# A transformer block in one kernel: jobs ordered by a table of ranks, input weights laid out piece by piece, a constant added inside a reduction

## The chip, the cores and the metric

The kernel runs on one core of a Trainium2 chip. The metric is the device time of one execution in microseconds (us); the median of several executions counts. The core has a matrix engine (TensorE, PE in the profile, with its weight loads as PEld), a vector engine (VectorE, DVE), an activation engine (ScalarE, ACT), a general engine (GpSimd, POOL) and SyncE (SP), which here issues every DMA. Each engine works through its own list of instructions in the order in which the program was written; semaphores hold an instruction until what it needs is done.

## The reference

```
scores = q @ k.T / 8, causal mask, softmax; attn = softmax @ v      # 4 batches, 12 heads, 448 positions, 64 wide
x  = attn, heads side by side                                       # 4 x 448 x 768
u  = x + (relu(x.T @ w_tok1) @ w_tok2).T                            # token mixing, 448 -> 256 -> 448
x  = u + relu(u @ w_ch1) @ w_ch2                                    # channel mixing, 768 -> 1536 -> 768
h  = relu(x @ w_in); a, v = halves of h                             # 768 -> 2 x 512
v  = (v - mean) / sqrt(var + 1e-6), over the 512 columns
out = (a * (w_spatial @ v + b_spatial)) @ w_out                     # 512 -> 768
```

Inputs of `q`, `k`, `v` are fp32; the weights arrive in 8-byte numbers and are narrowed to fp32 on the chip.

## The kernel before

Most products are made of three matmuls on fp32r operands: each operand is split into a high part (a cast, mostly on ACT) and a low part (the difference, on DVE or POOL), and high x high, high x low and low x high are summed in PSUM. That is `mm3` (lines 336 to 338), a helper, so that most matmuls of the profile carry one of these three lines. The low parts are made by `lo_part` (line 327) and the low part of a hidden value, with its relu, by `relu_lo` (line 330).

The work goes through these stages, which overlap. **Attention**: 24 pairs of heads; for each pair `scores` (matmuls, line 497; mask, scale and row maximum on DVE, line 506; exponential on ACT, line 523; the sum of a row gets 1e-9 added on DVE, line 534, and is inverted, line 535; rows are normalised on POOL, line 544), `transposed` (line 581, transposes on PE, copied out of PSUM on ACT or DVE, lines 585 and 584) and `weighted` (lines 669, 683 and 688). The last seven pairs are turned by DVE and a trip through DRAM instead. **Token mixing** follows every third pair (`token_mix`, with transposes on PE in line 741). **Weights**: a piece of the channel weights is loaded into the tile `way` (line 381), narrowed by three DVE instructions (`narrow`, lines 351, 353 and 355), stored to a DRAM tile `plain` (line 395), and later loaded again for a batch into a tile `whl` (`load_unit`, line 818), cast on ACT (line 819) and split on POOL (line 327). The gated part's weights go the same way (`gw`, lines 1105 and 1107). **Channel mixing** of batches 0 and 1 (`ch1`, with its relu on ACT in line 843 and `relu_lo` on DVE; `ch2`, whose result DVE adds to `U` in line 859), then of batches 2 and 3 together with seven products in place of eight (`seven`, `gather`, lines 997 to 1003 and 1080), then the gated part the same way, with the spatial product in lines 1355 and 1356 and its DVE steps in lines 1362 and 1363.

The order of the work is not that of the source. Every piece of work is a `Job` with an engine, a price in microseconds, the keys it reads and writes, the buffers it touches and a priority. `Plan.order` plays the jobs through a model of the engines (`Plan.run`): at each step it takes, among jobs that could start first, the one of the best priority. Priorities of the first pass come from formulas beside each job; then `Plan.due` walks backward from the end and gives each job its latest start as its priority, and the play is repeated, six passes in all (`PASSES`); the pass with the earliest end is used. In this model a DMA takes its bytes at 340 GB/s and 2.3 us more (`LANDING`), and a result reaches another engine after 0.1 to 0.25 us and PE 0.3 or 0.8 us later still. The play also picks PSUM banks, and for some copies whether ACT or DVE does them. The instructions of all five engines are then written out in the order of the modelled starts. Nothing is reordered on the chip.

Of the kernel before, what the change touches and what calls it, by code (L numbers as in the profile page):

```python
# [2 lines left out]

# [59 lines left out]
PASSES = 6  # L63
DUE = "ACT", "DVE", "POOL", "SP", "PE"
# [4 lines left out]
LANDING = 2.3  # L69

TOK_PRIO = 1.0

BLOCKS = 17


class Buf:


    def __init__(self, make, tag, prev=None, banks=None):
        self.make, self.tag, self.prev, self.banks = make, tag, prev, banks  # L80
        self.jobs, self.tile, self.left = [], None, 0

# [7 lines left out]
class Job:  # L90
    def __init__(self, eng, us, emit, prio, at, size, index, port, other):
        self.eng, self.us, self.emit, self.prio, self.at, self.size, self.index = eng, us, emit, prio, at, size, index
        self.other = other
        self.port = port or eng == "POOL"
        self.before, self.after, self.bufs = set(), [], set()


class Plan:
# [11 lines left out]
    def job(self, eng, us, emit, r=(), w=(), touch=(), prio=0.0, at=0.0, size=0, port=False, other=None):  # L110


        j = Job(eng, us, emit, prio, at, size, len(self.jobs), port, other)
# [16 lines left out]
        j.bufs |= set(touch)  # L130
        self.jobs.append(j)
        return j

    def order(self):
# [10 lines left out]
        own = {j: (j.eng, j.us, j.emit, j.prio) for j in self.jobs}  # L145
        best = None
        for k in range(PASSES):
            for j in self.jobs:
                j.eng, j.us, j.emit, _ = own[j]
            if not self.run():  # L150
                break
            end = max(j.start + j.us for j in self.jobs)
            if best is None or end < best[0]:
                best = end, [(j.start, j.eng, j.us, j.emit) for j in self.jobs], {b: b.tag for j in self.jobs for b in j.bufs if b.banks}
            self.due(end, own, k)
        for j, x in zip(self.jobs, best[1]):
            j.start, j.eng, j.us, j.emit = x
        for b, tag in best[2].items():
            b.tag = tag
        return sorted(self.jobs, key=lambda j: (j.start, j.index))  # L160

    def due(self, end, own, k):

        jobs = sorted(self.jobs, key=lambda j: (j.start, j.index))
        owners = {}
        for j in jobs:
            for b in j.bufs:
                if b.banks and b not in owners.setdefault(b.tag, []):
                    owners[b.tag].append(b)
        later = {}  # L170
        for l in owners.values():
            for b, c in zip(l, l[1:]):
                later[b] = [j for j in c.jobs if not j.before.intersection(c.jobs)]
        late, pe = {}, end
        for j in reversed(jobs):
            t = pe if j.eng == "PE" else end
            for a in j.after:
                lat = 0.0
                if a.eng != j.eng or j.eng == "SP":
                    lat = 0.25 if j.eng == "PE" else 0.1  # L180
                    if a.eng == "PE":
                        lat += 0.3 if j.start < START else 0.8
                if j.eng == "SP":
                    lat += j.size / 340e3 + LANDING
                t = min(t, late.get(a, end) - lat)
            for b in j.bufs:
                if j in b.jobs:
                    for a in later.get(b, ()):
                        t = min(t, late.get(a, end) - 0.3)
            late[j] = t - j.us  # L190
            if j.eng == "PE":
                pe = late[j]
        for j in self.jobs:
            if own[j][0] in DUE and own[j][3] < 1e8:
                j.prio = late[j]

    def run(self):
# [9 lines left out]
        free = dict.fromkeys(engines, 0.0)  # L207
        bank_free = [0.0] * 8
        dma = port_free = 0.0
        avail = {e: [] for e in engines}  # L210
# [8 lines left out]
        def start(j, e):  # L219
            s = max(free[e], j.ready, port_free if j.port else 0.0)  # L220
            for b in j.bufs:
                if b.banks and b.tag is None:
                    s = max(s, min(bank_free[i] for i in b.banks))
            return s

        done = 0
        while done < len(self.jobs):
            best = None
            for e in engines:
                if not avail[e]:  # L230
                    continue
                starts = [(start(j, e), j) for j in avail[e]]
                first = min(s for s, _ in starts)
                if first == inf:
                    continue
                s, j = min(((s, j) for s, j in starts if s <= first + 0.03), key=lambda x: (x[1].prio, x[1].index))
                if best is None or (s, j.prio) < (best[0] - 0.1, best[1].prio) or s < best[0] + 0.1 and j.prio < best[1].prio:
                    best = (s, j, e)
            if best is None:
                return False  # L240
# [6 lines left out]
            for b in j.bufs:  # L247
                if b.banks and b.tag is None:
                    b.tag = min(b.banks, key=lambda i: (bank_free[i] > s, -bank_free[i] if bank_free[i] <= s else bank_free[i]))
                    bank_free[b.tag] = inf  # L250
            j.start = s
            free[j.eng] = s + j.us
            if j.port:
                port_free = s + j.us
            end = s + j.us
            if j.eng == "SP":
                dma = max(dma, end) + j.size / 340e3
                end = dma + LANDING
            done += 1
            for b in j.bufs:  # L260
                if j in b.jobs:
                    b.left -= 1
                    if b.left == 0 and b.banks:
                        bank_free[b.tag] = end + 0.3
            for a in j.after:
                lat = 0.0
                if a.eng != j.eng or j.eng == "SP":
                    lat = 0.25 if j.eng == "PE" else 0.1
                    if a.eng == "PE":
                        lat += 0.3 if s < START else 0.8  # L270
                a.ready = max(a.ready, end + lat)
# [3 lines left out]
        return True  # L275
# [3 lines left out]
def mixer_kernel(ctx: ExitStack, tc: tile.TileContext, qkv, wtok, wch, wgv, wsp, bsp, out):  # L279
# [36 lines left out]
    def dve(n, psum=True):  # L316
        return (n * 1.05 + 60) / 1e3 if psum else (n * 1.09 + 40) / 1e3

    def pool(n, two=True):
        return (n * 2.35 + 60) / 1e3 if two else (n * 0.83 + 230) / 1e3  # L320
# [19 lines left out]
    def narrow(d, dk, w, wk, n, prio, banks=(3,)):  # L340
# [16 lines left out]
        for k in range(3):  # L357
            job("DVE", (n * 1.03 + 165) / 1e3, lambda k=k: step(k), r=[dk, (ps, 0)] if k else [dk], w=[wk] if k == 2 else [(ps, 0)], touch=[wk[0]], prio=prio)
# [10 lines left out]
    stats = [fixed(f"s{i}", [3, 8], F32, f"stats{i}") for i in range(4)]  # L369
# [5 lines left out]
    def convert(i, src, parts, prio, banks, keep=None):  # L375
# [5 lines left out]
        job("SP", 0.4, lambda: nc.sync.dma_start(b.t[:, : 2 * n], src.bitcast(U32)), w=[dk], prio=prio, size=n * 1024)  # L381
# [12 lines left out]
        if keep is not None:  # L394
            job("SP", 0.4, lambda: nc.sync.dma_start(plain[keep], b.t[:, 4 * HALF : 6 * HALF].bitcast(F32)), r=[(b, "w", x) for x in (False, True)], w=[("plain", keep)], prio=prio, size=393216)
# [1112 lines left out]
```

## Time and profile before

| | us |
|---|---|
| median of 3 executions | 760.67 |
| the three executions | 760.67, 758.09, 761.02 |
| the profiled execution, first to last instruction | 760.7 |
| PE busy in it | 747.2 |
| DVE busy | 622.3 |
| ACT busy | 427.4 |
| POOL busy | 298.2 |

The profiled execution's own time is its span: it agrees with the median of the three to a rounding, so nothing lies around the span that the trace doesn't show. The end of a matmul is modelled in the profile, and a matmul's row is longer than the distance to the next one, so PE's busy share hides short gaps; the distance between the starts of neighbours shows them.

### The profile page before, as it was taken

Reading aid. Unit: us, or ns where it says so; the run is one execution under the profiler, and the core shown is the slowest. Engines: PE = TensorE matmul, PEld = TensorE weight load, DVE = VectorE, ACT = ScalarE, POOL = GpSimd, SP = SyncE. Lnnn points to the kernel's source line nnn. Section 1 sums busy time; section 2 is a strip of 40 time slices with the busy share of each in tenths; the row PEclk is TensorE's granted clock in tenths of the full one; section 3 lists DMA queues with packets and bytes.
Section 4 is the critical chain, followed back from the end, with each engine's and each line's share of the span. In section 5 each row is a group of like instructions: output and inputs, shape, how many; then the busy total and the mean of one; then the engine's idle time right before and its main releaser. Section 6 shows DMA issues by size and latency. Waiting matters only on the chain. (4 is left out here: it accounts for less than half of the span.)

```text
span 760.7 us, 12440 instructions
## 1 busy us (share of the span) xinstructions
PE 747.2 (98%) x4216; PEld 640.3 (84%) x4216; DVE 622.3 (82%) x1512; ACT 427.4 (56%) x1040; POOL 298.2 (39%) x354
## 2 busy tenths in 40 slices
PE   8999999999989999999999999999999999999998
PEld 4577778888887888888889989998988888888997
DVE  6999599999867878876469978999999897599482
ACT  6998776445347765552336666654573665545241
POOL 4788764265494766563310000000420151542210
PEclk9999999999999999999999999999999999999999
DMA  6687158999976898898823122520301100400213
GB/s 228 207 285 238 55 163 316 335 318 333 339 225 190 298 307 250 234 304 220 241 84 117 39 84 84 187 84 1 118 22 42 43 0 1 132 1 28 83 49 133
DMA packets 48608, 122.02 MB, mean 160 GB/s; under 512 B 4896, under 2 KB 20256, under 8 KB 48032
## 3 DMA queue, kind: packets, MB, share of 16 engines
q1 hardware_dynamic: 48544, 121.23, 48.7%
q8 instruction: 33, 0.54, 0.3%
q14 instruction: 31, 0.25, 0.1%
HBM read 91.46 MB, written 29.75 MB: 159 GB/s over the span
## 5 line engine op out<-in xcount | busy, mean ns | idle before, releaser
L336 PE MATMUL psf<-fb,fa 128*128 128x448 f32 x420 | 154.0, 367 | 1.2 <-DVE hs L1001 0.6
L337 PE MATMUL psf<-fb,fa 128*128 128x448 f32 x420 | 153.7, 366 | 0.0
L338 PE MATMUL psf<-fb,fa 128*128 128x448 f32 x420 | 153.6, 366 | 0.0
L327 POOL TENSOR_TENSOR whl<-whl 128x768 fp32r<-128x768 f32 x45 | 83.2, 1851 | 89.5 <-ACT whl L819 89.4
L523 ACT ACTIVATE P<-P,stats 128x448 f32<-128x448 f32 (+3 forms) x192 | 96.1, 505 | 31.1 <-DVE stats L506 30.8
L544 POOL TENSOR_SCALAR P<-P,stats 128x448 f32<-128x448 f32 (+3 forms) x192 | 88.3, 483 | 38.1 <-DVE stats L535 30.8
L336 PEld LDWEIGHTS psf<-fb,fa 128*128 128x128 f32 x420 | 78.9, 188 | 9.2 <-DVE hs L1001 1.0
L337 PEld LDWEIGHTS psf<-fb,fa 128*128 128x128 f32 x420 | 78.9, 188 | 6.8
L338 PEld LDWEIGHTS psf<-fb,fa 128*128 128x128 f32 x420 | 78.9, 188 | 6.7
L506 DVE CUSTOM_DVE_ANT_0 P<-pss,mask 128x448 f32<-128x448 f32 (+3 forms) x192 | 70.9, 415 | 16.4 <-PE pss L497 16.0
L938 ACT CAST fa<-raw 128x384 fp32r<-128x384 f32 (+1 forms) x112 | 56.4, 531 | 42.7 <-DVE raw L951 21.6
L327 POOL TENSOR_TENSOR wv<-wf,wv 128x512 fp32r<-128x512 f32 x6 | 9.2, 1546 | 153.2 <-ACT wv L1156 153.2
L327 DVE TENSOR_TENSOR fa<-raw,fa 128x384 fp32r<-128x384 f32 (+1 forms) x109 | 61.0, 585 | 7.1 <-ACT fa L938 7.1
L336 PE MATMUL ps<-hid,whl 128*128 128x448 f32 x144 | 55.2, 383 | 3.1 <-DVE hid L330 1.9
L819 ACT CAST whl<-whl 128x768 fp32r<-128x768 f32 x45 | 37.4, 833 | 34.6 <-DMA whl<-plain 33.5
L336 PE MATMUL ps<-uhl,whl 128*128 128x448 f32 x144 | 55.6, 386 | 0.2 <-DVE U L859 0.2
L338 PE MATMUL ps<-hid,whl 128*128 128x448 f32 x144 | 53.3, 370 | 0.0
L337 PE MATMUL ps<-hid,whl 128*128 128x448 f32 x144 | 53.3, 370 | 0.0
L338 PE MATMUL ps<-uhl,whl 128*128 128x448 f32 x144 | 52.7, 366 | 0.0
L337 PE MATMUL ps<-uhl,whl 128*128 128x448 f32 x144 | 52.7, 366 | 0.0
L859 DVE TENSOR_TENSOR U<-ps,U 128x448 f32<-128x448 f32 x48 | 29.5, 619 | 20.9 <-PE ps L338 20.8
L327 POOL TENSOR_TENSOR ql<-stage,qh 128x896 fp32r<-128x896 f32 x18 | 38.1, 2116 | 14.9 <-issue 11.7
(174 smaller groups left out, 1793.2 us busy)
## 6 DMA issues: line engine op xcount, KB each, us to landing
way<-in_wch SPq DMA_DIRECT2D x24, 768.0 KB, 5.7
whl<-plain SPq DMA_DIRECT2D x45, 384.0 KB, 5.0
stage<-in_qkv SPq DMA_DIRECT2D x23, 448.0 KB, 4.7
plain<-way SPq DMA_DIRECT2D x24, 384.0 KB, 6.7
raw<-plain SPq DMA_DIRECT2D x24, 384.0 KB, 3.9
round<-PB SPq DMA_DIRECT2D x7, 1024.0 KB, 6.2
PT<-round SPq DMA_DIRECT2D x28, 256.0 KB, 6.2
v<-in_qkv SPq DMA_DIRECT2D x24, 256.0 KB, 4.1
```

Of the source, the lines that this page charges most:

```text
L327: e.tensor_tensor(lo, x, hi.bitcast(F32), op=ALU.subtract)
L336: nc.tensor.matmul(ps, ah, bh, start=(first and i == 0), stop=False, **kw)
L337: nc.tensor.matmul(ps, ah, bl, start=False, stop=False, **kw)
L338: nc.tensor.matmul(ps, al, bh, start=False, stop=(last and i == n - 1), **kw)
L506: nc.vector.tensor_tensor_reduce(out=P(i)[:M, j, :], in0=ps(i, j), in1=mask[:M, S - 128 : S - 128 + W] if j == 0 and n < BLOCKS or M == 64 ...
L523: nc.scalar.activation(P(i)[:M, j, :], P(i)[:M, j, :], AF.Exp, bias=s.t[:M, 0, c : c + 1], scale=-1.0, accum_out=s.t[:M, 1, c : c + 1])
L544: nc.gpsimd.tensor_scalar(P(i)[:M, j, :], P(i)[:M, j, :], s.t[:M, 2, c : c + 1], 1.0, op0=ALU.mult, op1=ALU.mult)
L819: job("ACT", act(DM, False), lambda: nc.scalar.copy(w.t[:, 0, :], w.t[:, 1, :].bitcast(F32)), r=ks, w=ks, prio=p)
L859: job("DVE", dve(S), lambda d=d, ps=ps: nc.vector.tensor_tensor(u.t[:, d, :], ps.t[:, :S], u.t[:, d, :], op=ALU.add), r=[(ps, 0), *u_keys( ...
L938: job("ACT", act(n, False), lambda: nc.scalar.copy(part(o, 0), at(d)), r=[key(d)], w=[wk], prio=p + 0.1 * o)
```

## The change

Three things are changed. First, the order: the six passes and `due` are removed, and each job's priority is read from a table of ranks, one number for each job, written into the source as text (`RANKS`); one play of the model follows. The model itself gets other prices: how late a result reaches each engine from each other one (`LAG`), a DMA's bytes at 290 to 415 GB/s behind a fixed 1.35 or 2.2 us from its issue, and for PE a kind of matmul for each job (`mode`: fp32r products and transposes 0, scores 1, weighted sums 2), with 0.09 us for a change of kind, a `lead` for the first product after a change or a wait, and a preference of 1.0 (`STAY`) for a job of the kind at hand. Prices of single jobs are set anew. Which instructions there are stays as it was, but for the choices that the play makes (bank, ACT or DVE) and the third part below.

Second, the layout in DRAM of three inputs. `in_wch`, `in_wgv` and `in_wtok` were arrays of 128 rows, and a piece was a range of columns of each row (rows of `in_wch` lie 147,456 bytes apart, and a piece takes 6,144 bytes of each); now each piece lies in one block. Sizes of the loads stay.

Third, the 1e-9 of the softmax's sum. Before, a DVE `tensor_scalar_add` (line 534) added it. Now the exponential writes its row sums into every second column of a strip, whose other columns are set to 1e-9 once at the start (four more small POOL memsets), and a DVE `tensor_reduce` adds neighbours; the reciprocal follows as before.

```
+STAY, NEAR, SLACK = 1.0, 0.03, 0.2
+LAG = {
+    "DVE": {"DVE": 0.123, "ACT": 0.118, "POOL": 0.168, "PE": 0.138, "SP": 0.11},
+    "ACT": {"DVE": 0.133, "ACT": 0.0, "POOL": 0.18, "PE": 0.155, "SP": 0.126},
...
+RANKS = (
...
-        own = {j: (j.eng, j.us, j.emit, j.prio) for j in self.jobs}
-        best = None
-        for k in range(PASSES):
...
-            self.due(end, own, k)
...
+        ranks = array("H", b85decode("".join(RANKS)))
+        assert len(ranks) == len(self.jobs)
+        for j, r in zip(self.jobs, ranks):
+            j.prio = r / 40
+        self.run()
         return sorted(self.jobs, key=lambda j: (j.start, j.index))
...
+            return min(((s, j) for s, j in starts if s <= first + NEAR), key=lambda x: (x[1].prio + (e == "PE" and x[1].mode != mode) * STAY, x[1].index))
...
+            if e == "PE":
+                waited = s > free[e] + 0.03
+                if j.mode != mode and not waited:
+                    s += 0.09
+                if j.mode == 0 and (waited or mode):
+                    us += j.lead
+                mode = j.mode
...
-            if j.eng == "SP":
-                dma = max(dma, end) + j.size / 340e3
-                end = dma + LANDING
+            if e == "SP":
+                free[e] = s + 0.385
+                dma = end = max(dma, s + (1.35 if j.mode else 2.2)) + j.size / (j.lead * 1e6)
...
-    stats = [fixed(f"s{i}", [3, 8], F32, f"stats{i}") for i in range(4)]
+    stats = [fixed(f"s{i}", [4, 8], F32, f"stats{i}") for i in range(4)]
+
+    def sums(s):
+        return s.t[:, 2:4, :].rearrange("p x c -> p (x c)").rearrange("p (c x) -> p c x", x=2)
...
-                nc.vector.tensor_scalar_add(s.t[:, 2, cols], s.t[:, 1, cols], 1e-9)
-                nc.vector.reciprocal(s.t[:, 2, cols], s.t[:, 2, cols])
+                nc.vector.tensor_reduce(s.t[:, 1, cols], sums(s)[:, cols, :], axis=mybir.AxisListType.X, op=ALU.add)
+                nc.vector.reciprocal(s.t[:, 1, cols], s.t[:, 1, cols])
...
+    def piece(x, o, n):
+        return x[128 * o : 128 * (o + n)].rearrange("(p n) -> p n", n=n)
...
-        convert(i % 3 if i < 6 else 1 + i % 2, wch[:, i * DM : i * DM + DM], parts, LOW + i, (7,) if i < 8 else (3,), keep=i)
+        convert(i % 3 if i < 6 else 1 + i % 2, wch[i], parts, LOW + i, (7,) if i < 8 else (3,), keep=i)
...
     for s in stats:
         nc.gpsimd.memset(s.t, 0.0)
+        nc.gpsimd.memset(sums(s)[:, :, 1:2], 1e-9)
...
-    wch = np.concatenate([first[u[1]] if u[0] == 1 else second[u[1], u[2]] for u in UNITS], axis=1)
+    wch = np.stack([first[u[1]] if u[0] == 1 else second[u[1], u[2]] for u in UNITS])
...
+    wgv = in_pieces(wgv, [HALF] * 8 + [FF] * KM + [HALF] * 8)
+    wtok = in_pieces(wtok, (768, 704, 448))
```

## Rows read from the trace of the kernel before

**Rows 1.** The page: span, and busy time of the matrix engine

```profile
span 760.7 us, 12440 instructions
PE 747.2 (98%) x4216; PEld 640.3 (84%) x4216; DVE 622.3 (82%) x1512; ACT 427.4 (56%) x1040; POOL 298.2 (39%) x354
```

**Rows 2.** Stretches: length, busy PE, PEld, DVE, ACT, POOL; clock, DMA share, GB/s

```profile
20.00:50.00 30.00, 28.40 (x219) 18.70 (x216) 27.39 (x108) 30.00 (x96) 24.09 (x45) 1.00 0.76 251
...
100.00:215.00 115.00, 111.74 (x658) 94.56 (x658) 106.25 (x252) 60.19 (x145) 61.25 (x68) 0.99 0.89 308
500.00:600.00 100.00, 99.43 (x471) 88.02 (x471) 97.93 (x207) 53.24 (x120) 14.04 (x18) 1.00 0.16 50
```

**Rows 3.** Who PE waited for: idle us in total, times, longest

```profile
PE ps L336 <- DVE U L859: 1.2, 2, 1.1
PE psp L1355 <- DVE gate L1363: 0.9, 2, 0.7
...
PE psf L336 <- DVE hs L1001: 0.6, 1, 0.6
PE psf L336 <- DVE U L1080: 0.6, 1, 0.6
```

**Rows 4.** Timeline, all engines, about the longest wait: start, length, instruction, [idle before]

```profile
208.00 0.36 PE L338 MATMUL ps<-uhl,whl 128*128 128x448 f32 x1
...
209.82 0.37 PE L338 MATMUL ps<-hid,whl 128*128 128x448 f32 x1
210.02 0.83 ACT L819 CAST whl<-whl 128x768 fp32r<-128x768 f32 x1 [1.93 <-DMA whl<-plain]
210.76 0.54 ACT L843 ACTIVATE hid<-ps 128x448 fp32r<-128x448 f32 x1
...
211.45 0.62 DVE L330 SCALAR_TENSOR_TENSOR hid<-ps,hid 128x448 fp32r<-128x448 f32 x1
...
212.13 0.47 PE L336 MATMUL ps<-hid,whl 128*128 128x448 f32 x1 [1.94 <-DVE hid L330]
...
212.43 0.36 PE L337 MATMUL ps<-hid,whl 128*128 128x448 f32 x1
```

**Rows 5.** The stretch right behind that wait; columns as in the other stretches

```profile
213.10:216.50 3.40, 3.40 (x11) 3.05 (x10) 3.25 (x7) 2.59 (x4) 3.40 (x6) 0.50 0.58 201
```

**Rows 6.** Timeline of PE: first and last change of kind, and two changes

```profile
4.09 1.18 PE L497 MATMUL pss<-stage 64*64 64x64 f32 x8
...
184.73 0.37 PE L338 MATMUL ps<-hid,whl 128*128 128x448 f32 x1
185.03 0.42 PE L497 MATMUL pss<-qh 64*128 64x320 f32 x2
...
390.32 0.45 PE L336 MATMUL ps<-hid,whl 128*128 128x448 f32 x1
390.61 0.37 PE L337 MATMUL ps<-hid,whl 128*128 128x448 f32 x1
390.81 0.36 PE L338 MATMUL ps<-hid,whl 128*128 128x448 f32 x1
```

**Rows 7.** Who ACT waited for between 100 and 215 us

```profile
ACT whl L819 <- DMA whl<-plain: 15.4, 12, 4.6
```

**Rows 8.** Timeline of SP: two loads of channel weights are issued

```profile
110.10 0.33 SPq L381 DMA_DIRECT2D way<-in_wch  x1
...
114.37 0.33 SPq L381 DMA_DIRECT2D way<-in_wch  x1
```

**Rows 9.** The stretches in which their bytes move; columns as before

```profile
111.00:114.20 3.20, 3.20 (x24) 2.25 (x21) 3.06 (x8) 1.48 (x5) 1.04 (x1) 1.00 0.96 249
...
117.60:119.80 2.20, 2.20 (x15) 1.97 (x14) 2.13 (x7) 1.10 (x2) 1.55 (x1) 1.00 1.03 424
```

**Rows 10.** Line 534, the added constant: shortest, median, longest, in ns

```profile
L534 DVE TENSOR_SCALAR stats<-stats x25: 127/166/1702, 8.7 to 335.4; 128x8 f32<-128x8 f32 x23, 128x4 f32<-128x4 f32 x2
```

**Rows 11.** Timeline of POOL: its first work behind the memsets

```profile
9.30 3.13 POOL L544 TENSOR_SCALAR P<-P,stats 128x192 f32<-128x192 f32 x7 [6.20 <-DVE stats L535]
```

More of the change, by code (lines that the diff above doesn't have):

```diff
@@ L1 @@
+from array import array
+from base64 import b85decode
 from contextlib import ExitStack
 from functools import partial
+from itertools import count
 import concourse.bass as bass
@@ L76 @@
+NUMBER = count()
 class Buf:
@@ L81, in __init__ @@
         self.jobs, self.tile, self.left = [], None, 0
+        self.number = next(NUMBER)
     @property
@@ L108, in buf, with job @@
         return b
-    def job(self, eng, us, emit, r=(), w=(), touch=(), prio=0.0, at=0.0, size=0, port=False, other=None):
-        j = Job(eng, us, emit, prio, at, size, len(self.jobs), port, other)
+    def job(self, eng, us, emit, r=(), w=(), touch=(), prio=0.0, at=0.0, size=0, port=False, other=None, mode=0, lead=0.1):
+        j = Job(eng, us, emit, prio, at, size, len(self.jobs), port, other, mode, lead)
         for k in r:
@@ L156, in order @@
[L156 to L159, printed above, removed]
-        return sorted(self.jobs, key=lambda j: (j.start, j.index))
[L162 to L182, printed above, removed]
-                if j.eng == "SP":
[L184 to L195, printed above, removed]
@@ L197, in run @@
+        for j in self.jobs:
+            j.after.sort(key=lambda a: a.index)
+            j.of = [b for b in j.bufs if j in b.jobs]
+            j.banked = [b for b in j.bufs if b.banks]
+        ranks = array("H", b85decode("".join(RANKS)))
[3 more added lines that the diff above has]
+        self.run()
+        return sorted(self.jobs, key=lambda j: (j.start, j.index))
     def run(self):
@@ L217, in run, with look @@
                 add(j)
[L219 to L224, printed above, removed]
+        def look(e):
+            f, starts, first = free[e], [], inf
+            for j in avail[e]:
+                s = j.ready if j.ready > f else f
+                if j.port and port_free > s:
+                    s = port_free
+                for b in j.banked:
+                    if b.tag is None:
+                        k = sum(c.tag is None and c.banks == b.banks for c in j.banked)
+                        s = max(s, sorted(bank_free[i] for i in b.banks)[k - 1])
+                starts.append((s, j))
+                if s < first:
+                    first = s
+            if first == inf:
+                return None
+            return min(((s, j) for s, j in starts if s <= first + NEAR), key=lambda x: (x[1].prio + (e == "PE" and x[1].mode != mode) * STAY, x[1].index))
         done = 0
@@ L229, in run @@
             for e in engines:
-                if not avail[e]:
+                x = look(e) if avail[e] else None
+                if x is None:
                     continue
[L232 to L236, printed above, removed]
+                s, j = x
                 if best is None or (s, j.prio) < (best[0] - 0.1, best[1].prio) or s < best[0] + 0.1 and j.prio < best[1].prio:
                     best = (s, j, e)
-            if best is None:
-                return False
             s, j, e = best
@@ L983, in weight_factors @@
             for k, unit in enumerate((i, i2)):
-                job("SP", 0.4, lambda t=t, k=k, unit=unit: nc.sync.dma_start(t.t[:, k, :], plain[unit]), r=[("plain", unit)], w=[(t, k, x) for x in range(2)], prio=base + z, size=393216)
+                job("SP", 0.385, lambda t=t, k=k, unit=unit: nc.sync.dma_start(t.t[:, k, :], plain[unit]), r=[("plain", unit)], w=[(t, k, x) for x in range(2)], prio=base + z, size=393216, lead=0.415)
             split_weights(HALF, at, key, lambda o, x, z=z: w[o].t[:, z, x], lambda o, z=z: (w[o], z), base + z, WEIGHT_LO_DVE)
@@ L1036, in seven @@
                     after += start
-                job("PE", 0.607 * n, mms, r=[*after, us[z][1](o), *((*place[o][i][:2], x) for i in range(n) for x in range(2))], w=[(ps, 0)], prio=base + 0.01 * o)
+                job("PE", (0.0, 0.0, 1.216, 1.842)[n], mms, r=[*after, us[z][1](o), *((*place[o][i][:2], x) for i in range(n) for x in range(2))], w=[(ps, 0)], prio=base + 0.01 * o)
                 done(z, o, ps)
```

203 lines of the change are left out of this document (127 added, 76 removed).

## The prediction

> **What bounds the kernel now.** I read the page first: PE is busy for 747.2 of 760.7 us [rows 1], and no other engine comes near. So only time in which PE does nothing, or does its work slowly, can be won; the products themselves stay. The page's busy share hides part of that, so three more views follow. In the table of stretches the reader is to see where PE is not full and who is full there instead: between 20 and 50 us PE misses 1.60 us and ACT is busy for all 30.00; between 100 and 215 us PE misses 3.26 us while DVE is busy for 106.25 of 115 and the DMA engines for 89%; between 500 and 600 us PE misses 0.57 us and DVE is busy for 97.93 [rows 2]. The list of PE's waits names who ended them [rows 3]. The timeline then shows how one comes about, and what it costs in full.
>
> The longest is plain. The last product of a hidden unit starts at 208.00, so ACT could do its relu (line 843) soon after 208.4. But ACT's list has a cast of a weight tile in front of it (line 819), and that cast waits for its DMA: ACT stands for 1.93 us, casts at 210.02, and the relu starts only at 210.76. DVE's `relu_lo` follows at 211.45, and PE, which ran out of other products at 209.82, goes on at 212.13 [rows 4]. Nothing was short of an engine: the relu was queued behind a late load. From start to start PE took 2.31 us, then 0.30 us, where 0.20 is its pace [rows 4, 6]: it lost 2.21 us, 0.27 more than the 1.94 listed as idle. And right behind it the granted clock stood at 0.50, the lower of the two levels, 1.2 GHz, for 3.40 us [rows 5].
>
> **The change part by part.** The instructions stay, so the sum is made of what PE loses now, and how much of each loss a new order, or earlier data, can take away.
>
> *The waits in channel mixing, 190 to 217 us.* Three waits: the one above (1.94) and two on DVE's line 859 (1.2 together) [rows 3, 4], with 0.27 for each beyond the listed idle: 3.9 us. The low clock halves the work of 3.40 us: 1.7 more. Together 5.6 us. What attacks them is both the order (a relu in front of a cast whose data is late costs nothing) and the landing of the data. The lower bound of the gain is nothing, the upper 5.6; I take 4.7, because the cause seen in the row is a matter of order alone, and this is what a table can set.
>
> *The layout of the weights.* Its price has to be read from DMA. A load of `way` is 768 KB. One, issued at 110.10, moves at 249 GB/s between 111.0 and 114.2 with the DMA engines busy for 96%; the next, issued at 114.37, moves at 424 GB/s [rows 8, 9]. So 3.2 us against 1.9: 1.3 us a load, and for 24 loads between nothing and 31 us of DMA time, most of it before 215 us, where DMA is 89% busy [rows 2]. None of it is PE's time by itself. It counts through what queues on the same engines: ACT's casts wait 15.4 us for `whl` in that stretch, 12 times [rows 7], and the longest wait of PE lies behind one of them [rows 4]. So it is part of the 4.7 above, and I add nothing. If the loads stay as slow as they are, the order alone remains there; then I would take 3.0 instead of 4.7.
>
> Two loads of one pitch at such different rates also say that pitch alone doesn't explain the slow one. The Trainium skill, page "DMA: Bandwidth & Descriptors", section "Latency and other measured facts", ties slow HBM streams to row pitches at large powers of two (from 512 KiB) and advises contiguous tiles; 147,456 bytes is no power of two. By that rule this layout need not help, and the forecast would be the one with 3.0, 1.7 us later.
>
> *The other waits of PE.* Two on the gate's DVE work (0.9), one on line 1001 and one on line 1080 (0.6 each) [rows 3]: 2.1, with 0.27 for each 3.2 us. I take 1.3: in the stretch that holds one of them DVE is 98% busy [rows 2], so there a different order mostly moves the wait. Bounds 0 and 3.2.
>
> *The first 50 us.* PE's 1.60 us between 20 and 50 stand against an ACT that is never idle [rows 2]. A new order can only hand copies from ACT to DVE (27.39 of 30.00 busy). I take 0.8; bounds 0 and 1.6.
>
> *Changes of kind on PE.* Going from products to scores takes 0.30 us from start to start in place of 0.20, and the first product behind transposes 0.29 [rows 6]: 0.1 us each. Between the first at 4.09 and the last at 390.32 there are 183 such changes. A third of them lead into transposes, which show no such step, so about 12 us is spent so. At least three runs a pair must stay (scores, transposes, weighted sums, with the softmax in between): 72 of 183. So at most 111 could go, two thirds of them at 0.1 us: 7.4 us. The preference for the kind at hand holds only among jobs whose ranks are within 1.0 of each other, so I take 2.2; bounds 0 and 7.4.
>
> *The constant.* Line 534 runs 25 times, at 166 ns in the median but up to 1,702 ns [rows 10]. A reduction of this shape is not in the trace; if it costs the median, the gain is the long ones, at most 1.5 us each of DVE's time; if it cost 0.3 us, it would lose 25 times 0.13, 3.4 us of DVE's 622.3. PE doesn't wait on it by any row, and the pair's normalisation on POOL hides it; should that cover be gone, once 1.5 us either way. I take nothing. The Trainium skill, page "SBUF — State Buffer", section "Who interferes with whom", says that `tensor_scalar` can take the port pair shared with GpSimd, one then blocking the other wholly, and that `tensor_reduce` never does on this chip; it would explain the 1,702 ns, which the row alone does not, and by it the sum is the same. The four memsets at the start stand before POOL's first work, which waits 6.20 us until 9.30 [rows 11]: nothing, unless they took 1.5 us each.
>
> The sum: 4.7 + 1.3 + 0.8 + 2.2 = 9.0 us, from 760.7 to 751.7. I say 751.5.
>
> **The rivals.** *New waits in the place of the old (slower).* The table fixes the order for one set of prices, and in it a load lands on time. Where one is later, whatever stands behind its consumer on ACT or DVE is late, and PE with it, as at 210 us: 2.2 us, and 1.7 if the clock falls: 3.9 each time. ACT waits for `whl` 12 times between 100 and 215 us [rows 7], and at least one of these reaches PE now [rows 4]. If the old ones stay in kind (no 4.7) and the other 4.3 are won, two more such waits (7.8) decide: 764.2, and with three it is 768.1. For it: DMA is 89% busy there, so landings scatter, as the two rates show [rows 2, 9]. Against it: the new prices don't lean on one pace for all loads, and contiguous pieces can only scatter less.
>
> *The waits only move (no change).* DVE is 92% busy from 100 to 215 us and 98% from 500 to 600, ACT full from 20 to 50 [rows 2]. If PE's waits are set by these engines and not by their order, only the changes of kind are won: 760.7 - 2.2 = 758.5. Against it: at 208 us neither engine was short [rows 4].
>
> *More than I take.* All of the waits go (5.6 + 3.2 + 1.6) and half of the possible changes of kind (3.7): 760.7 - 14.1 = 746.6. For it: nothing in the products themselves forbids it. Against it: a search finds such an order in its own prices, and the chip's landings scatter.
>
> **How the numbers follow.** The forecast (746 to 756.9) gets 0.62, 0.20 of it with loads as slow as before (3.0 in place of 4.7: 753.4); more than that (below 746) 0.10, waits that only move (756.9 to 764.5) 0.17, new waits (above) 0.11. The 0.5% that tell a change from none are 3.8 us here: faster below 756.9, slower above 764.5. So faster 0.72, same 0.17, slower 0.11. The range takes in most of the larger gain (all bounds together, 5.6 + 3.2 + 1.6 + 7.4 = 17.8, would give 742.9) and the case of no change up to 762: 743 to 762. The forecast's own range is 746.6 to 756.
>
> **What would show it.** Right, if the profile after has PE's idle time between 100 and 215 us below 1 us, no granted clock below full there, and relus on ACT that no longer follow a cast which waited for DMA; if the loads of `way` move at 380 GB/s and more; if the changes of kind along PE number some 160 or fewer; if the reduction shows no runs over 0.3 us. Wrong, if the list of PE's waits has as much in it under new names, if the clock falls somewhere after a gap that wasn't there, or if PE's busy time shrinks by far more than the changes of kind can give: then I have missed a cost inside the products.

## The result, and the profile after

The changed kernel takes 766.53 us in the median of ten executions (763.29 to 770.28), the kernel before 760.60 us (758.09 to 763.44, ten executions): ratio 1.0084, interval 1.0067 to 1.0102. It is slower by some 6 us, and the forecast of 751.5 us and its range are missed. The slower rival, new waits in the place of the old, is what came in kind; its two prices were 764.2 and 768.1 us.

A plain correction first: the profiled execution of the kernel after has a time of 766.04 us and a span of 764.2, and the 78 executions of the kernel before that were timed beside the later runs show 1.7 to 1.9 us between the two as well. So something does lie around the span, and that the span of before (760.7) met its median is a coincidence: the profiled execution of before took about 762.5 us (an estimate: span plus 1.8), 1.9 above that kernel's median. The two profiles are therefore 3.5 us apart, where the medians are 5.9 apart.

The page of the kernel after, span and busy times:

```profile
span 764.2 us, 12383 instructions
PE 747.8 (98%) x4216; PEld 638.5 (84%) x4216; DVE 618.2 (81%) x1525; ACT 424.4 (56%) x1027; POOL 293.1 (38%) x358
```

Against [rows 1] every engine but PE has less to do (DVE 4.1 us, ACT 3.0, POOL 5.1), PE about the same, and the span is 3.5 us longer. No work was added; PE waits more. The same stretches as in [rows 2]:

```profile
20.00:50.00 30.00, 29.50 (x233) 18.75 (x232) 28.46 (x117) 29.12 (x97) 25.23 (x46) 1.00 0.62 205
100.00:215.00 115.00, 111.05 (x653) 94.91 (x651) 97.65 (x233) 54.97 (x131) 55.28 (x55) 1.00 0.84 279
500.00:600.00 100.00, 98.18 (x464) 86.46 (x463) 97.19 (x202) 52.20 (x115) 14.54 (x18) 1.00 0.16 51
```

Between 20 and 50 us PE now misses 0.50 (before 1.60): that gain came. Between 100 and 215 it misses 3.95 (before 3.26), though DVE is less busy than before. Between 500 and 600 it misses 1.82 (before 0.57). The list of PE's waits, beside [rows 3] (the `zeros` line is a warm-up that both kernels have):

```profile
PE pss L542 <- DMA stage<-in_qkv: 2.9, 2, 1.9
PE zeros L1469 <- DVE P L1466: 1.4, 1, 1.4
PE pst L626 <- ACT PT L630: 1.4, 2, 1.2
PE ps L378 <- DVE U L907: 1.3, 3, 0.6
PE pss L542 <- DVE way L397: 1.1, 1, 1.1
PE psf L378 <- DVE U L1128: 1.1, 1, 1.1
PE psf L378 <- ACT v L1237: 0.7, 1, 0.7
```

The 1.9 us on `hid` is gone, and other names stand in its place. One of them, in the timeline (start, length, instruction, idle before it), is the old case again:

```profile
180.34 1.57 ACT L867 CAST whl<-whl 128x768 fp32r<-128x768 f32 x2 [2.77 <-DMA whl<-plain]
...
180.94 0.34 PE L380 MATMUL psm<-xs,wt 128*128 128x384 f32 x1
...
181.82 0.58 ACT L630 COPY PT<-pst 128x512 f32<-128x512 f32 x1
...
182.45 0.66 PE L626 MATMUL pst<-ident,P 128*128 128x128 f32 x4 [1.17 <-ACT PT L630]
```

PE has its transposes in PSUM and wants them copied out; ACT has two casts in front of that copy, and stands 2.77 us because their load is late. It is [rows 4] with a copy where the relu was. ACT's waits for `whl` over the whole kernel grew from 33.5 us (19 times) to 46.5 (this sum alone decides little: run e5 below has 46.9 and loses far less):

```profile
ACT whl L867 <- DMA whl<-plain: 46.5, 24, 7.3
```

DVE, busy for 81% and the engine that ends most of PE's waits, shows it more plainly. It stands for DMAs 16.6 us in the kernel after and 4.9 us in the kernel before; the longest sums of each (after, then before):

```profile
DVE psw L393 <- DMA way<-in_wch: 8.5, 9, 1.6
...
DVE PB L654 <- DMA round<-PB: 3.7, 3, 1.8
DVE psw L393 <- DMA gw<-in_wgv: 3.7, 5, 1.8
...
DVE psw L351 <- DMA gw<-in_wgv: 2.7, 5, 1.1
DVE psw L351 <- DMA way<-in_wch: 1.5, 2, 1.1
```

**How typical the old stall was.** The prediction's largest term is read from the wait and the low clock behind 208 us [rows 4, 5]. Two stretches in the profiles of before, of e1 (below: the old order again, with the new layout and constant, as fast as before) and of after:

```profile
60.00:160.00 100.00, 99.72 (x688) 81.16 (x689) 86.25 (x242) 65.59 (x176) 57.22 (x70) 1.00 0.69 231
60.00:160.00 100.00, 99.72 (x690) 81.22 (x689) 84.40 (x239) 65.39 (x176) 56.66 (x70) 1.00 0.69 230
60.00:160.00 100.00, 96.90 (x636) 78.30 (x636) 82.98 (x226) 58.80 (x152) 55.70 (x64) 1.00 0.79 259
...
190.00:217.00 27.00, 23.74 (x106) 20.66 (x105) 22.58 (x45) 11.63 (x20) 15.63 (x15) 0.94 0.90 314
190.00:217.00 27.00, 26.04 (x125) 22.50 (x124) 24.48 (x49) 12.18 (x23) 17.25 (x17) 1.00 0.95 333
190.00:217.00 27.00, 26.21 (x134) 23.25 (x133) 22.52 (x43) 9.44 (x16) 13.76 (x15) 1.00 0.81 270
...
PE ps L336 <- DVE hid L330: 0.6, 1, 0.6
```

In 190 to 217 us PE misses 3.26 at a mean clock of 0.94 in the profile of before, but 0.96 at full clock in e1, whose wait on `hid` is 0.6 us (the last line). The mean granted clock of before's profiled execution was 0.997; of the 78 other executions of that kernel 71 have 0.999 or 1.000 (median 760.28 us), and only 7 have 0.997 or 0.998 (762.45 us). So at least the low clock was a matter of few executions, and there was little of it to win in the median. The new loss lies elsewhere: between 60 and 160 us the kernel after misses 3.10, the old order 0.28 in both profiles.

Three more rows for parts of the prediction. In this execution a stretch of low clock lies at the start, behind the wait of 1.9 us for `stage` (six of after's ten executions have a mean clock of 1.000); the stretches in which two loads of `way`, now contiguous, move differ as in [rows 9]; and the reduction has no long runs (shortest, median, longest, to be set beside [rows 10]):

```profile
11.30:14.70 3.40, 3.40 (x11) 1.60 (x8) 3.33 (x20) 2.98 (x13) 2.55 (x6) 0.50 0.90 328
...
85.50:88.10 2.60, 2.60 (x15) 2.31 (x16) 2.53 (x5) 0.81 (x2) 2.14 (x5) 1.00 1.02 414
114.50:117.90 3.40, 3.40 (x23) 2.95 (x23) 3.20 (x6) 0.95 (x2) 0.00 (x0) 1.00 0.89 248
```

```profile
L579 DVE TENSOR_REDUCE stats<-stats x25: 117/161/171, 11.6 to 322.5; 128x8 f32<-128x16 f32 x23, 128x4 f32<-128x8 f32 x2
```

**Where the time went.** For each matmul I take the time that its kind needs at pace (202.5 ns for 448 columns, for instance) and sum them along PE: what the clock shows at T beyond that sum is lost by then. The differences in lost time between two profiles, in us (plus: the first has lost more):

| until (us) | 20 | 60 | 160 | 210 | 220 | 300 | 450 | 600 | end |
|---|---|---|---|---|---|---|---|---|---|
| after less before | 3.0 | 1.0 | 4.2 | 4.7 | 1.5 | 1.5 | 2.1 | 2.9 | 3.5 |

So 3 us go at the start, most of them come back by 60 us, 3.7 more are lost in many small waits up to 210, the stall that the profiled execution of before had behind 208 us is won (3.2), and 0.8 go between 450 and 600. (With other choices of pace the entries move by up to about 1 us; the signs stay.) Against e1's profile, whose span is 757.8 us, that win is all but absent: counted in the same way, after has lost 3 to 5 us more at 220 us and 6.4 at the end.

**Landings against prices.** Both models give each DMA a landing. For 306 DMAs I compare the time from issue to landing with what the model has for it, queue included. In the kernel before the chip is earlier than the price by 0.62 us in the median, and later by 1.05 at the ninth decile. In the kernel after it is later by 0.25 in the median, and by 1.48 at the ninth decile. The DMAs themselves changed little (from issue to landing `way` took 5.7 us in the median and now 6.2, `whl` 5.0 and now 4.5). The old prices were too dear and left room; the new ones are fair in the middle and leave none for the late half.

### The profile page after: what moved, and what is told of

Same layout as the page of the kernel before. It is cut to its first block, busy times and chain, and to the rows that moved or that the text cites. A ratio compares the mean times of both kernels' runs of the same rounds, so it can differ in the third digit from the quotient of the medians.

```text
span 764.2 us, 12383 instructions
## 1 busy us (share of the span) xinstructions
PE 747.8 (98%) x4216; PEld 638.5 (84%) x4216; DVE 618.2 (81%) x1525; ACT 424.4 (56%) x1027; POOL 293.1 (38%) x358
## 4 chain that ended last, share of the span: by engine, by line
PE 70%; DVE 11%; DMA 7%; ACT 2%; issue 1%; SPq 0%; DVEq 0%; ACTq 0%
PE psf L378 11%; PE psf L379 11%; PE psf L380 11%; PE ps L378 6%; PE ps L380 5%; PE ps L379 5%; DMA way<-in_wch 4%; PE pss L542 2%; PE psv L379 2%; PE psv L380 2%; PE psv L378 2%; PE pst L626 2%; PE pso L714 2%; PE psm L378 2%; PE psm L380 1%; PE psm L379 1%
## 5 line engine op out<-in xcount | busy, mean ns | idle before, releaser
L589 POOL TENSOR_SCALAR P<-P,stats 128x320 f32<-128x320 f32 (+3 forms) x192 | 87.8, 474 | 41.9 <-DVE stats L580 36.7
L378 PEld LDWEIGHTS psf<-fb,fa 128*128 128x128 f32 x420 | 78.8, 188 | 11.2 <-issue 1.4
L551 DVE CUSTOM_DVE_ANT_0 P<-pss,mask 128x192 f32<-128x192 f32 (+3 forms) x192 | 71.1, 413 | 14.8 <-PE pss L542 13.7
L986 ACT CAST fa<-raw 128x384 fp32r<-128x384 f32 (+1 forms) x112 | 56.3, 532 | 45.0 <-DVE raw L999 23.1
L867 ACT CAST whl<-whl 128x768 fp32r<-128x768 f32 x45 | 37.2, 834 | 51.8 <-DMA whl<-plain 46.5
L626 PE MATMUL pst<-ident,P 128*128 128x128 f32 x272 | 39.4, 277 | 2.7 <-ACT PT L630 1.4
```

Source lines behind the costliest of these rows:

```text
L378: nc.tensor.matmul(ps, ah, bh, start=(first and i == 0), stop=False, **kw)
L551: nc.vector.tensor_tensor_reduce(out=P(i)[:M, j, :], in0=ps(i, j), in1=mask[:M, S - 128 : S - 128 + W] if j == 0 and n < BLOCKS or M == 64 ...
L589: nc.gpsimd.tensor_scalar(P(i)[:M, j, :], P(i)[:M, j, :], s.t[:M, 1, c : c + 1], 1.0, op0=ALU.mult, op1=ALU.mult)
L626: nc.tensor.transpose(ps.t[:, c : c + 128], src, ident)
L867: job("ACT", act(DM, False), lambda: nc.scalar.copy(w.t[:, 0, :], w.t[:, 1, :].bitcast(F32)), r=ks, w=ks, prio=p)
L986: job("ACT", act(n, False), lambda: nc.scalar.copy(part(o, 0), at(d)), r=[key(d)], w=[wk], prio=p + 0.1 * o)
```

## The experiments

Theory A: the order loses because it was made for loads that land on time. Theory B: the loss has other reasons (layout, constant, or lists that are worse whatever the loads do). Each run is timed against the kernel before on the same chip.

**Which part of the change.** e1 is the kernel before with the new layout and constant; e2 the new order, table and prices alone:

```
-            convert(i, piece(wtok, a, cuts[-1]), parts, TOK_PRIO + 0.1 * i, (7,))
+            convert(i, wtok[:, a : a + cuts[-1]], parts, TOK_PRIO + 0.1 * i, (7,))
...
-                nc.vector.tensor_reduce(s.t[:, 1, cols], sums(s)[:, cols, :], axis=mybir.AxisListType.X, op=ALU.add)
+                nc.vector.tensor_scalar_add(s.t[:, 2, cols], s.t[:, 1, cols], 1e-9)
```

(so e2 against after, e1 the other way round against before).

> The kernel before, its order untouched (six passes, old prices), with the two other parts of the change: the inputs in pieces and the 1e-9 inside a reduction. Theory A (the order is the whole loss, the other two parts are hidden): within 1.5 us of the kernel before, about 760.6. Theory B (the new layout or the reduction slows something, for instance loads that land later): 764 us or more.

> The new table of ranks and the new prices, with the old layout of the inputs and the old added constant. Theory A (the order is the whole loss): 766 us, within 1.5 us of the changed kernel. Theory B (layout or reduction): 760 to 762.

Measured: e1 759.92 us, ratio 0.9994 (0.9978 to 1.001); e2 768.28 us, ratio 1.0097 (1.007 to 1.0125). The order is the whole loss. Layout and constant change nothing measurable in the old order; e2 is 1.8 us above after, a little more than its 1.5.

**The start alone.** e3 gives the first six DMAs of SP their old order (the `v` loads last), which is where the table of lost time begins:

```
+        sp = sorted((j for j in self.jobs if j.eng == "SP"), key=lambda j: (j.start, j.index))[:6]
+        starts = [j.start for j in sp]
+        for j, s in zip(sorted(sp, key=lambda j: j.size == 262144), starts):
+            j.start = s
```

> The changed kernel, with only the first six DMAs on SP in the old order: all the q and k loads of pairs 0 and 1 ahead of both v loads. In the changed kernel PE waits 1.91 us at 9.6 us for pair 1's load. If the start is a good part of the loss: 1.5 to 2.9 us less than the changed kernel, some 764. If the softmax's engines make up for the late start anyway: within 0.7 us of the changed kernel, 766.5.

Measured: 766.05 us, ratio 1.0063 (1.0035 to 1.009). In its profile the 1.9 us are won at 20 us and held until 220, and by 400 all are lost again in waits that after did not have. The wait at the start is real, but winning it changed the time by nothing that can be told from noise; that an order with no room in it doesn't hand the time through is my reading.

**Less DMA time, and more.** e4 and e5 halve the loads of `way` and `gw` in both kernels; e6 and e7 put a copy that nobody reads ahead of each load of `way` and `whl`. No list of another engine changes.

```
e5
-        job("SP", 0.385, lambda: nc.sync.dma_start(b.t[:, : 2 * n], src.bitcast(U32)), w=[dk], ...
+        job("SP", 0.385, lambda m=n if keep is None or keep < 3 else HALF: nc.sync.dma_start(b.t[:, : 2 * m], src[:, :m].bitcast(U32)), w=[dk], ...
e7
+    def with_copy(load):
+        nc.sync.dma_start(spare.pop(), wch[0][:, :256])
+        load()
```

> The kernel before, but 21 of the 24 loads of way and most loads of gw bring only the first half of their columns (the other half of the tile keeps the piece before, so those weights are wrong; every instruction of the other engines stays). It takes DMA time away without touching any list. Theory A (the order of the change loses because it has loads land earlier than the chip lands them, the old order was made with later landings in its prices): the old order gains little, 755 to 760 us. Theory B (landings have no part in it; the new lists of ACT and DVE are worse whatever the loads do): the same here, 755 to 760 us. This run is the yardstick for the next.

> The changed kernel with the same loads halved in the same way (those weights wrong again). Theory A: with the loads landing as early as the new prices say, the new order loses its late landings and is at least as fast as the old one with halved loads: 752 to 759 us, not more than 1 us above the run beside it. Theory B: it stays 5 to 8 us above the run beside it, 761 to 767 us.

> The kernel before with one more DMA ahead of each load of way and of whl: 128 rows of 2,048 bytes from an input to a DRAM tile that nothing reads. It waits for nothing; each load is issued some 0.35 us later and lands later by its bytes. Theory A: the old order has room for it, 3 to 12 us slower than before, 763 to 772 us. Theory B: the same here; the yardstick for the next.

> The changed kernel with the same copies ahead of the same loads. Theory A: the new order has no room for later landings, so the distance to the old one grows from 6 us to more than 12: 778 to 800 us. Theory B: the distance stays at 5 to 8 us, 768 to 780 us.

| | before's order | after's order | distance |
|---|---|---|---|
| halved loads (e4, e5) | 757.94 | 760.17 | 2.2 |
| as they are | 760.60 | 766.53 | 5.9 |
| more DMA (e6, e7) | 769.39 | 795.45 | 26.1 |

The ratios to before are 0.9972 (0.9954 to 0.999), 0.9998 (0.9982 to 1.0013), 1.0131 (1.0097 to 1.0165) and 1.0472 (1.0446 to 1.0499). Nothing but the DMA queue was touched, and the distance between the orders goes from 2 to 26 us: theory A in its core. DVE's standing for DMAs goes along: 0.9 us in e4, 4.9 in before, 12.8 in e6; in the new order 4.5 in e5, 16.6 in after, 37.5 in e7. And the loss between 60 and 160 us, 3.10 in after, is 0.90 in e5:

```profile
60.00:160.00 100.00, 99.10 (x655) 81.07 (x654) 85.87 (x235) 60.87 (x160) 57.94 (x67) 1.00 0.65 208
```

What the runs don't separate is which old price gave the room. With the landings the change also cut what a result needs on its way to PE (0.1 us and 0.3 or 0.8 more before; 0.1 to 0.16 and a `SLACK` of 0.2 after); no run gave one of the two back alone. ACT's waits for `whl` in e7, and PE's longest, with the names they had:

```profile
ACT whl L872 <- DMA whl<-plain: 81.8, 34, 7.6
```

```profile
PE ps L378 <- DVE U L912: 6.0, 2, 3.8
PE pst L631 <- DVE U L840: 3.4, 2, 1.9
PE pss L547 <- DVE way L397: 2.2, 1, 2.2
```

But A had asked for e5 to be no more than 1 us above e4, and it is 2.2 us above (barely clear of the noise). With halved loads the landings are on the price (0.03 us late in the median), and the profile of e5 is 3.4 us ahead of e4's at 210 us (that execution of e4 is 2.3 us above e4's median); it gives back 2.9 between 450 and 600, where the DMA engines are 20% busy (PE waits 1.6 there for `U`, line 1128, and 0.7 for `v`, line 1237). So there is a second cause, which isn't late loads. What it is, the rows only suggest. The wait for `U` in the kernel after:

```profile
552.36 2.87 POOL L369 TENSOR_TENSOR wv<-wf,wv 128x512 fp32r<-128x512 f32 x2 [2.85 <-ACT wv L1204]
552.73 1.35 DVE L369 TENSOR_TENSOR fa<-raw,fa 128x384 fp32r<-128x384 f32 x1 [0.24 <-ACT fa L986]
554.00 0.61 DVE L1128 TENSOR_TENSOR U<-psf,U 128x448 f32<-128x448 f32 x1
554.53 1.18 DVE L955 TENSOR_TENSOR U<-U,U 128x448 f32<-128x448 f32 x1
...
555.64 1.14 DVE L1128 TENSOR_TENSOR U<-psf,U 128x448 f32<-128x448 f32 x2
...
556.39 0.44 PE L378 MATMUL psf<-fb,fa 128*128 128x448 f32 x1 [1.07 <-DVE U L1128]
```

While POOL works on two tensors, DVE's `fa` takes 1.35 us (0.55 in the median) and the addition `U<-U,U` 1.18; `U<-psf,U`, one of whose operands is in PSUM, takes its 0.61. DVE is 1.4 us late in a stretch where it has no slack, and PE waits 1.07. The other wait there has neither POOL nor a DMA in it: ACT's copy of `v` starts late at 590.29, behind two casts in its list.

```profile
589.35 1.03 ACT L950 CAST fb<-U 128x448 fp32r<-128x448 f32 x2 [0.33 <-DVE U L955]
...
590.29 0.59 ACT L1237 ACTIVATE v<-psv 128x512 f32<-128x512 f32 x1
...
590.93 0.47 PE L378 MATMUL psf<-fb,fa 128*128 128x448 f32 x1 [0.65 <-ACT v L1237]
```

Long DVE instructions beside POOL stand in every profile: I count for DVE's instructions what they take beyond the median of their kind, where that is over 0.25 us. It is 8.1 us in after and 11.2 in before, and every one of them runs while POOL has work. So this sum alone doesn't explain the loss, since the faster kernel has more of it; what counts is whether PE waits behind it.

**An order made for late loads.** If A holds, a search over the same model in which landings scatter should give an order that keeps its gain. e8 to e10 write the order out job by job:

```
-        return sorted(self.jobs, key=lambda j: (j.start, j.index))
+        return [self.jobs[i] for i in array("H", b85decode("".join(ORDER)))]
```

> The changed kernel, its order written out job by job, with only those jobs of ACT, DVE and POOL moved that wait for a DMA: 309 of 1,147 change places with others in their engine's list, 306 of them counted with direction: 92 later and 62 earlier on ACT, 200 and 91 on DVE, 14 and 4 on POOL. The places come from a search over the model of the changed kernel in which each landing is between 0.4 us earlier and 2.6 us later than its price (12 draws). If all landings were on time, the model has this order 1.5 us slower than the change's. Theory A (readers of loads stand too early in the lists, and what is behind them is late with them): most of the loss comes back, 757 to 762 us. Theory B (the loss lies in the rest of the order): no gain, 764 to 769 us.

(Its total is wrong: of the 1,147 jobs that wait for a DMA, 306 stand later among the others and 157 earlier, 463 together.)

> The changed kernel with all jobs free to move (their banks and the choice of ACT or DVE stay), searched over the same model with the same 12 draws of late landings, from the change's order. Theory A: an order that is found with landings scattered keeps its gain on the chip: 751 to 757 us, faster than before. Theory B (a search over this model fits the model and not the chip, whatever the landings are): 759 to 768 us.

> The kernel before with its order written out in the same way and searched over the same model and draws from the old order; old layout and old constant. Theory A: 752 to 758 us. Theory B: 759 to 768 us.

Measured: e8 766.61 us, ratio 1.0069 (1.0044 to 1.0093), no gain against after; e9 755.22 us, ratio 0.9929 (0.9909 to 0.9949); e10 766.89 us, ratio 1.0084 (1.0059 to 1.0108). One hit, two misses. e9 beats both kernels; the stretches of its profile, to be set beside those of after:

```profile
20.00:50.00 30.00, 29.84 (x237) 18.92 (x236) 28.91 (x114) 29.61 (x100) 25.84 (x44) 1.00 0.67 225
100.00:215.00 115.00, 114.87 (x687) 100.22 (x686) 100.30 (x239) 56.46 (x133) 63.89 (x59) 1.00 0.84 280
500.00:600.00 100.00, 99.70 (x473) 88.20 (x472) 94.83 (x199) 52.45 (x126) 16.02 (x21) 1.00 0.22 78
```

PE misses 0.13 us of 115 where it missed 3.95, with DMA as busy as in after. DVE stands for DMAs 2.4 us, not 16.6, ACT waits 25.9 us for `whl`, not 46.5, and six executions lie within 1.0 us of each other, those of after within 7.0. The start is as it was: PE misses 4.21 in the first 20 us, in after 4.52. e10 loses 5.0 us or more at one place, and that place is the old constant:

```profile
80.07 4.42 DVE L592 TENSOR_SCALAR stats<-stats 128x8 f32<-128x8 f32 x1 [2.15 <-ACT P L581]
80.61 2.09 POOL L385 TENSOR_TENSOR ql<-stage,qh 128x896 fp32r<-128x896 f32 x1
...
82.67 1.79 POOL L385 TENSOR_TENSOR whl<-whl 128x768 fp32r<-128x768 f32 x1
84.52 0.20 DVE L593 RECIPROCAL stats<-stats 128x8 f32<-128x8 f32 x1
84.64 0.58 DVE L749 COPY U<-pso 128x448 f32<-128x448 f32 x1
...
85.37 0.45 PE L639 MATMUL pst<-ident,P 128*128 128x128 f32 x1 [3.67 <-DVE U L749]
```

An instruction of 8 columns holds DVE for 4.42 us, until the second of two back-to-back POOL instructions ends; PE waits 3.67 us, and the granted clock is 0.50 for 6.8 us:

```profile
84.60:91.40 6.80, 6.03 (x18) 5.49 (x19) 2.14 (x5) 0.53 (x1) 3.64 (x8) 0.50 0.11 46
```

e8, in its profiled execution (769.12 us, the longest of seven), fails first by a load later than any of the draws (2.6 us at most): one of `gw`, issued at 153.61, lands 8.0 us later with the DMA engines busy for 91%, some 4.6 us behind its price in the comparison above; DVE stands 3.90 us for it, and PE 2.8. And its DVE loses 18.5 us beside POOL in the count above, against 8.1 in after; in e10 it is 23.1.

**The constant by itself, and the good order again.** e11 is e10 with the `tensor_reduce`, e12 is e9 with the old `tensor_scalar_add` (the edits shown for e2, one of them reversed); e13 and e14 are e9's search with other draws.

> The run e10_before_scattered with one edit: the constant is added by the tensor_reduce of the change. In e10 one tensor_scalar of the old constant took 4.42 us at 80.07 while POOL worked without a gap, and PE lost 5.0 us there against the kernel before. Theory C (that run's loss is the old constant, which waits for POOL, and not its order): 759 to 763 us. Theory B (the searched order is bad on the chip in any case): 765 to 768 us.

> The run e9_after_scattered (755.2 us) with one edit: the constant is added by the old tensor_scalar. Theory C: its 25 runs are short but where POOL has work without a gap; some 5 of them are long by 3 to 8 us of DVE's time together, and one or two reach PE: 757 to 762 us. Theory D (the constant costs nothing in an order that has slack): 754.5 to 756 us.

> As e9_after_scattered, from the change's order with the change's banks, with another seed and 24 other draws of late landings. Theory A (searching with landings scattered is what helps): again faster than before, 753 to 758 us. Theory E (e9 was a lucky order; orders of such a search scatter by their collisions of DVE with POOL, which the model lacks): anywhere from 756 to 767 us, not faster than before in the mean of this run and the next.

> As e13, with a third seed and 12 further draws. Theory A: 753 to 758 us. Theory E: as said there.

| | us | ratio to before |
|---|---|---|
| e11 | 758.50 | 0.9986 (0.9968 to 1.0003) |
| e12 | 758.89 | 0.9984 (0.9961 to 1.0007) |
| e13 | 758.17 | 0.9963 (0.9947 to 0.998) |
| e14 | 757.44 | 0.9975 (0.9962 to 0.9988) |

e11: the constant was worth 8.4 us in that order, more than the 5.0 of the one place; its six long runs in e10 add up to 8.0 us. Even so e11 can't be told from before: the search from the old order won nothing that is clear of the noise. e12: the constant costs 3.7 us in e9's. Of its 25 runs four are long (3.3 us together), and 2.4 us are lost by 350 us in the profiled execution (760.66 us, 1.8 above e12's median); the other 3.6 come behind 386 to 393 us, where two DVE instructions run beside POOL for 2.3 us each, PE then waits 2.1 us and has 3.4 us at a granted clock of 0.50, and no constant stands near. Whether the shift that the constant made brought these together, one profile doesn't say. e13 and e14: faster than before both times, 8 to 9 us faster than after, but 2 to 3 us short of e9. (Against the ranges stated for them, e11 lies 0.5 us below and e13 0.2 above.) Three searches out of three that started from the change's order with late landings beat both kernels. That the late landings are what helped, and not the further search, is theory A's reading and isn't shown: no run searched as long with landings on time. Why e9 is ahead is open as well. The long DVE instructions beside POOL come to 14.0 and 12.7 us in e13 and e14 and to about 10 in e9; the model keeps POOL and those DVE instructions apart by a common `port`, the constant excepted, but on the chip they meet where times differ from the prices.

## Why the prediction was wrong

*The step that failed* is the largest term, 4.7 of 5.6 us for the waits in channel mixing, with its reason: "the cause seen in the row is a matter of order alone, and this is what a table can set". The row showed two things, a late load and a relu behind its reader. Two things were wrong with it. The 5.6 us were the cost of one profiled execution, and taken as the kernel's: against that profile the stretch of 190 to 217 us did win 2.5 us of idle time and the low clock (0.79 missed in place of 3.26, clock 1.00 in place of 0.94), but e1's profile of the old order misses 0.96 there at full clock, so some 0.2 us were left to win. And the sum has no term for what a table costs when loads are late. A table can set the place of a relu behind its reader only for the lateness that it knows: between 60 and 160 us, where the old order misses 0.28, the new one misses 3.10, with DVE standing for DMAs 16.6 us in all in place of 4.9. In the stretch that the prediction named as the sign, 100 to 215, PE's idle time is 3.95: 0.7 more than in the profile of before, 1.6 more than in e1's 2.32.

*The rival "new waits"* named this mechanism and had 764.2 and 768.1; it got 0.11. That 766.5 lies between its prices is in part luck: it counted two or three waits of 3.9 us with a fall of the clock between 100 and 215 us and 4.3 us won elsewhere, and what came are many small waits and little won. What the text held against it, "the new prices don't lean on one pace for all loads, and contiguous pieces can only scatter less", was wrong in both halves: the new prices leave no room (late by 0.25 in the median where the old ones were early by 0.62), and the pieces scatter as before. The rival needed a fast landing to be *bad to plan for*, and the diff showed it: the fixed part went from 2.3 us behind the bytes to 1.35 or 2.2 ahead of them, and bytes at up to 415 GB/s in place of 340. That could be weighed against the 249 GB/s of [rows 9].

*The layout* was priced at nothing in itself, rightly (e1), but I took the faster loads for granted in 4.7. The loads of `way` land 4.5 to 8.7 us after their issue, 6.2 in the median (before 4.5 to 8.1, and 5.7). The price of 1.3 us a load was read too high as well: the GB/s of a stretch are those of all queues, and the packets of the two loads in [rows 9] (6,144 bytes each) by themselves took 3.39 and 2.40 us, a difference of 1.0. The rule of the Trainium skill that the prediction cited (page "DMA: Bandwidth & Descriptors", section "Latency and other measured facts"), by which this layout need not help, agrees with this.

*The other waits* (1.3) were not won but exchanged: 1.82 us missed between 500 and 600 against 0.57, on `U` and on `v`. *The first 50 us*: 1.10 won between 20 and 50, more than the 0.8 taken, but 3.0 lost before 20 on `stage`, in a place that the prediction didn't look at. *Changes of kind* (2.2): 184 in place of 183, so next to nothing won. The count took transposes as a kind of their own, and the change's `mode` has them as one with the products: by `mode` the changes did fall, from 120 to 96, while those between products and transposes, which the preference doesn't see, rose from 61 to 86.

*The constant* at nothing was right for the old order and for this change. Its bound was not: "at most 1.5 us each" came from the longest run in one profile, and another order made it 4.42, with 8.4 us for the whole kernel (e10, e11). The rule cited from the page "SBUF — State Buffer" of the Trainium skill, that `tensor_scalar` can be kept out by GpSimd and `tensor_reduce` never, agrees: 4,424 ns for the one, 173 ns at most for the other in the kernels that had it. Its section is "Who interferes with whom".

What stays open: how the 5.9 us divide. Halving the loads takes 3.7 us of them away. The rest, 2.2, lies mostly between 450 and 600 us, where the rows show DVE beside POOL and a copy behind two casts; no run changed either alone.

## What to carry to other kernels

An order whose plan leaves no room behind a load hands late loads on to the bottleneck engine: the same extra DMAs cost the old order 8.8 us and the new one 28.9. So judge a plan by what some lateness does to it, not by its end alone; searching against scattered landings gave faster orders three times out of three from this start. Before a wait is priced from one profile, ask in how many executions it stands. Replace small instructions that can be held off by another engine even where they cost nothing now: the next order may put them in front of something.

## What the runs showed of the hardware that was not expected

A DVE `tensor_scalar` of 128x8 elements waited through two POOL instructions in a row (2.09 and 1.79 us) and did not get in between them: 4.42 us in e10 for what takes 0.17. DVE's `tensor_tensor` of 448 columns with both operands in SBUF was stretched too (2.32 for 0.62 us in e12); with one operand in PSUM none that overlapped POOL took more than 0.633 us, in any of the 16 profiles. Loads of 384 KB on one queue took from 2.9 to 8.0 us to land within one execution (`whl` in after, 4.5 in the median).
